# Sliding-window attention and a two-layer product on one core: the written order of steps is replaced, the steps of both products get explicit names, and chunk 1 of the first layer uses its three PSUM banks turned by one

## The chip, the cores and the metric

The kernel runs on one core of one Trainium2 chip. The metric is device time in microseconds (us) of one execution, lower is better. Three runs of the kernel before gave 321.90, 321.86 and 319.94 us; their median is 321.86 us.

## The reference

```python
# q, k, v: (8 batches, 8 heads, 576 tokens, 64)
scores = q @ k^T / 8
mask = (rel >= 0) & (rel < 64)            # rel = query position - key position
attn = softmax(where(mask, scores, -1e9))
x = (attn @ v) as (4608 tokens, 512)      # heads side by side
h = x @ w_in                              # w_in: 512 x 2048
y = (h - tanh(h)) @ w_out                 # w_out: 2048 x 512
```

All of it is float32 outside; the matrix products run in bf16 with float32 sums in PSUM.

## The kernel before

**Work.** Heads are handled in pairs: pair `g` (0 to 31) is two heads of batch `g // 4`. A window is 64 tokens; a batch has nine. The tokens of all batches stand in one row of 72 windows, cut into nine chunks of eight (512 tokens). A batch therefore ends inside a chunk: batch 4 supplies the last four windows of chunk 4 and the first five of chunk 5.

**Order.** Nothing is scheduled by the framework. A text, `PLAN`, is a list of words; `play` goes through it from left to right and issues each step on its engine. Each engine runs its own queue in that order and waits only for semaphores, so the text fixes the order on every engine, and the place of a word matters only against the other words of the same engine. The waits follow from the tiles: a step waits for what writes what it reads, and also for earlier steps that still use what it overwrites. The overlap is judged by the tile's region, and it counts by the place in the text: a fill that stands behind a load into the same tile waits for the load's landing, one that stands before the load does not.

The words that this document uses:

- `lk.g.p`, `lq.g.p`, `LQ.b`, `lr.b.i.h`, `LV.b.i`, `lv.b.pr.half`, `lt.b`, `wi.i`, `wo.i`: loads issued by GpSimd (POOL): keys and queries of a pair, queries of a batch, key rows of block `i` of a batch, rows of V, parts of V of batch 1, the two weight matrices. `lk.0.s` and `lq.0.s` go by SyncE (SP). Loads of POOL use eight semaphores in turn, so each waits until the one eight places before it has landed.
- `mv.i` fills the ones column and the empty first block of V buffer `i` (`vw`); `mk`, `mt`, `mq`, `h`, `i`, `n`, `z` fill other constants; `z` clears two large query buffers `qz` on POOL (`more_zeros`).
- `za`, `zb` and `Z.b` copy V across the partition halves (`Z` is two copies on VectorE, `cross_rows`). `cz.g` copies queries into `qz` (POOL), `bo.g` writes them to DRAM, `td.g` and `tk.b.i` are transposing DMAs of SP that give queries and keys.
- `ck`, `cq` cast keys and queries; `Fp`, `Ep` transpose them on TensorE; `Fc`, `Ea`, `Eb`, `Ec` take them out of PSUM. The last letter of such a word is the engine: `a` ScalarE, `v` VectorE, `p` GpSimd.
- `Rp.g.grp.bank` are scores, `Rx` their exponential (ScalarE), `M.g` the mask on the result (VectorE), `P`/`PP` the product with V for one or two pairs, `D` or `DR`, `DN` the division by the sum (VectorE).
- `Xp`, `Xc` transpose a batch's result into the chunk tiles by TensorE (batches 0 to 2); from batch 3 on `Y.b` does it by two transposing DMAs of SP, one for each chunk that the batch lies in.
- `H.c.m` is one of 16 blocks of the first layer for chunk `c` (four matmuls of 128x512, `hp_mm`), `A` its tanh on ScalarE (`squash`), `G` the subtraction on VectorE (`g_sub`). `W.c.s.part` is a quarter of the second layer for 128 tokens (`yp_mm`), `O.c.s` the copy out and the store (`y_out`). Before the change these five words carry no numbers: `step` counts how often each has come up and takes the next block.

**PSUM.** `ps` has eight banks. The first layer uses banks 0, 1 and 2 in chunks 0 and 1 and banks 0 and 1 from chunk 2 on, so `H` waits for the subtraction of the block two or three places earlier. The second layer uses banks 2 and 0 in chunk 0, bank 2 in chunks 1 to 7, banks 0 and 2 in the last. Scores use bank 4 (for the first four pairs 0, 1 and 4, 7), transposes banks 2 and 3, products with V banks 5 to 7.

Of the kernel before, what the change touches and what calls it, by code (L numbers as in the profile page):

```python
# [15 lines left out]
def kernel(  # L16
# [10 lines left out]
    B, H, S, D = q.shape  # L27
# [452 lines left out]
    FIRST = [(0, m, s) for s in range(2) for m in range(SPLIT)] + [(0, m, None) for m in range(SPLIT, M)]  # L480

# [3 lines left out]
    def hp_mm(c, m, s):  # L485
        n = columns(s)
        hp = ps[:, m % 2 if c > 1 or s is not None else m % 3, n]
        for ki in range(4):
            nc.tensor.matmul(hp, w_in_tile(ki, m),  # L489
                             chunk_tile(c)[:, n.start // 64:n.stop // 64, ki % 2, 64 * (ki // 2):64 * (ki // 2) + 64],  # L490
                             start=(ki == 0), stop=(ki == 3))
        return hp
# [15 lines left out]
    def yp_mm(c, st):  # L508
        s, part = divmod(st, 4)
        if c == 0:  # L510
            s, part = 2 * (st // 8) + st % 2, st % 8 // 2
        if c == NC - 1 and s == 3:
            half = part // 2
            d = slice(half * (d_model // 2), (half + 1) * (d_model // 2))
            for m in range(8 * (part % 2), 8 * (part % 2) + 8):
                nc.tensor.matmul(ps[:, 2 - half, d], gT[c][:, m, s * 128:(s + 1) * 128], w_out_sb[:, m, d],  # L516
                                 start=(m == 0), stop=(m == M - 1))
            return
        yp = ps[:, yp_bank(c, s), :]
        for i in range(4):  # L520
            m = 4 * part + i
            nc.tensor.matmul(yp, gT[c][:, m, s * 128:(s + 1) * 128], w_out_sb[:, m, :],  # L522
                             start=(m == 0), stop=(m == M - 1))
# [31 lines left out]
    def first_layer():
        k = step("H")
        hidden[k] = hp_mm(*k)

    def tanh():
        k = step("A")  # L560
        hidden[k] = squash(k[2], hidden[k])

    def subtract():
        k = step("G")
        g_sub(*k, *hidden.pop(k))
# [18 lines left out]
        H=first_layer, A=tanh, G=subtract, W=lambda: yp_mm(*step("W")), O=lambda e: y_out(*step("O"), e))  # L584

    def play(script):
# [103 lines left out]
```

## Time and profile before

| what | value |
|---|---|
| runs | 321.90, 321.86, 319.94 us, median 321.86 |
| span of the profiled execution | 317.8 us, so 4.1 us less than the median run |
| mean granted TensorE clock | 0.995 |
| TensorE matmul busy | 305.3 us (96%), 2412 matmuls |
| VectorE, ScalarE, GpSimd busy | 187.8, 173.2, 111.7 us |
| first layer (L489) | 576 matmuls, 140.2 us busy |
| second layer (L522) | 560 matmuls, 135.9 us busy |
| DMA | 39.11 MB, engines at 90% or more in nearly all of the first half |

The page shows one execution. Its span runs from the first to the last instruction; no time of its own is printed for that execution, and what a run takes beyond the span is start and end, the 4.1 us above. A busy TensorE does not mean a TensorE at its peak, since matmuls overlap: two matmuls of 128x512 that follow each other start 0.216 us apart, though each is listed with 0.379 us. How long TensorE really stood is therefore read from the starts of its instructions.

### The profile page before, as it was taken

How to read it: one execution, taken by the hardware profiler on the slowest of the kernel's cores; microseconds unless marked ns; L12 is line 12 of the kernel's file. 1: busy time of each engine (PE TensorE's matmuls, PEld its weight loads, DVE VectorE, ACT ScalarE, POOL GpSimd, SP SyncE). 2: the span in 40 equal slices, each digit the busy share in tenths (PEclk: the TensorE clock that was granted, in tenths of full speed). 3: DMA queues.
4: the chain of work that ended last, by engine and by line, in shares of the span. 5: the costliest groups of instructions: out<-in, count | busy, mean ns of one | idle time of the engine just before them, and what ended most of it. 6: DMA issues, size and time to landing. Idle time of an engine off the chain costs nothing.

```text
span 317.8 us, 6105 instructions
## 1 busy us (share of the span) xinstructions
PE 305.3 (96%) x2412; PEld 165.7 (52%) x2412; DVE 187.8 (59%) x321; ACT 173.2 (54%) x322; POOL 111.7 (35%) x164
## 2 busy tenths in 40 slices
PE   7878999999999999999799999999999999999995
PEld 2455565656655655555455555555554544445444
DVE  2355995489887896769374666566753554244400
ACT  4678885589778675555344635544524435334311
POOL 8982849985871384892021430000000000000000
PEclk9799999999999999999999999999999999999999
DMA  9999999999999699999998999262014010010021
GB/s 151 152 202 198 190 196 130 181 154 146 155 138 166 99 138 151 188 148 119 199 156 157 136 166 206 72 144 72 33 36 107 33 68 33 33 36 33 33 99 68
DMA packets 113133, 39.11 MB, mean 123 GB/s; under 512 B 96336, under 2 KB 107600, under 8 KB 113104
## 3 DMA queue, kind: packets, MB, share of 16 engines
q0 software_dynamic: 72064, 18.06, 66.4%
q1 hardware_dynamic: 41040, 20.65, 31.4%
q8 instruction: 19, 0.31, 0.4%
q14 instruction: 10, 0.08, 0.1%
HBM read 36.70 MB, written 11.80 MB: 153 GB/s over the span
## 4 chain that ended last, share of the span: by engine, by line
PE 86%; DMA 5%; DVE 4%; ACT 3%; issue 1%; SPq 0%; ACTq 0%; DVEq 0%
PE ps L489 37%; PE ps L522 36%; PE ps L300 4%; DMA xT<-xs 3%; PE ps L261 3%; PE ps L418 3%; PE ps L225 1%; DMA qf<-in_q_dram 1%; PE ps L516 1%; DVE xs L447 1%; PE ps L453 1%; ACT qt L88 1%; DVE qt L90 1%; DVE vw L167 1%; ACT pt L305 1%
## 5 line engine op out<-in xcount | busy, mean ns | idle before, releaser
L489 PE MATMUL ps<-xT,wi 128*128 128x512 bf16 x576 | 140.2, 379 | 2.4 <-DMA xT<-xs 1.7
L503 DVE TENSOR_TENSOR gT<-ps,th 128x512 bf16<-128x512 f32 x144 | 97.9, 689 | 72.5 <-ACT th L497 68.3
L522 PE MATMUL ps<-w_out_sb,gT 128*128 128x512 bf16 x560 | 135.9, 379 | 0.0
L497 ACT ACTIVATE th<-ps 128x512 f32<-128x512 f32 x144 | 85.3, 598 | 74.7 <-PE ps L489 70.9
L489 PEld LDWEIGHTS <-wi 128*128 128x128 bf16 x576 | 62.6, 113 | 53.6 <-DMA xT<-xs 1.8
L522 PEld LDWEIGHTS <-gT 128*128 128x128 bf16 x560 | 52.9, 98 | 55.3
L305 ACT ACTIVATE pt<-ps 128x384 bf16<-128x384 f32 (+1 forms) x92 | 46.0, 504 | 24.5 <-PE ps L300 23.0
L176 POOL DMA_DIRECT2D kall<-in_k_dram x50 | 37.2, 753 | 11.0 <-DMA vw<-in_v_dram 4.7
L160 POOL DMA_DIRECT2D vw<-in_v_dram x35 | 30.1, 866 | 12.3 <-PE ps L300 11.9
L88 ACT ACTIVATE ysb<-ps 128x512 f32<-128x512 f32 (+1 forms) x25 | 14.6, 582 | 29.4 <-PE ps L522 26.8
L393 DVE TENSOR_TENSOR pt<-pt,ps 128x1152 bf16<-128x1152 bf16 x28 | 20.7, 746 | 4.0 <-ACT pt L305 4.0
L128 POOL COPY qz<-qall 96x384 bf16<-96x384 bf16 x16 | 7.6, 517 | 41.4 <-DMA qd<-qz 35.7
L300 PEld LDWEIGHTS <-kw 128*128 128x128 bf16 x180 | 14.3, 98 | 10.9
L300 PE MATMUL ps<-qt,kw 128*128 128x128 bf16 x180 | 19.7, 219 | 0.0
L88 ACT ACTIVATE qt<-ps 64x576 bf16<-64x576 bf16 x25 | 16.1, 643 | 3.0 <-PE ps L300 1.5
L438 DVE TENSOR_TENSOR xs<-ps,rcp 128x384 bf16<-128x384 f32 x28 | 15.1, 552 | 0.3
L90 DVE COPY qt<-ps 64x576 bf16<-64x576 bf16 x15 | 11.3, 755 | 3.5 <-PE ps L261 2.0
L90 DVE COPY ysb<-ps 128x512 f32<-128x512 f32 x12 | 8.2, 685 | 7.9 <-PE ps L522 7.9
L418 PEld LDWEIGHTS <-pt 128*64 128x64 bf16 x504 | 9.2, 111 | 4.6 <-issue 2.4
L225 PE MATMUL ps<-warm 128*128 128x512 bf16 x25 | 10.1, 552 | 1.3 <-DVE warm L206 1.1
L418 PE MATMUL ps<-vw,pt 128*64 128x65 bf16 x504 | 10.7, 197 | 0.4 <-DVE vw L167 0.4
L261 PE MATMUL ps<-ident,qb 96*128 96x96 bf16 x132 | 9.6, 210 | 0.4 <-DVE qb L90 0.3
(68 smaller groups left out, 167.6 us busy)
## 6 DMA issues: line engine op xcount, KB each, us to landing
out_dram<-ysb SPq DMA_DIRECT2D x35, 256.0 KB, 2.3
vw<-in_v_dram POOLq DMA_DIRECT2D x28, 128.0 KB, 5.9
qall<-in_q_dram POOLq DMA_DIRECT2D x5, 576.0 KB, 8.9
kall<-in_k_dram POOLq DMA_DIRECT2D x40, 64.0 KB, 5.8
qd<-qz SPq DMA_DIRECT2D x8, 288.0 KB, 4.1
w_out_sb<-in_moe_w_out_dram POOLq DMA_DIRECT2D x4, 512.0 KB, 8.5
kall<-in_k_dram POOLq DMA_DIRECT2D x11, 144.0 KB, 5.1
qall<-in_q_dram POOLq DMA_DIRECT2D x11, 144.0 KB, 5.2
```

The costliest lines, as they stand in the source:

```text
L88: nc.scalar.activation(o, i, ACT.Copy)
L90: eng.tensor_copy(o, i)
L160: nc.gpsimd.dma_start(out=w[:, 2 * i + 1, :, 0:D] if i < NF else w[64:128, 2 * i, :, 0:D], in_=v[b, :, 128 * i:128 * i + n].rearrange("h p ...
L176: nc.gpsimd.dma_start(out=token_rows(b)[0:c, i, :, h, :], in_=k[b, NP * h:NP * h + NP, 128 * i:128 * i + c].rearrange("r p d -> p r d"))
L300: nc.tensor.matmul(sp[:, i], kt[:, 64 * j:64 * j + 128], qT[g % NR][:, :, 64 * j:64 * j + 64], start=first, stop=first or i == n - 1)
L305: nc.scalar.activation(PT[g % NPT][:, js[0]:js[0] + len(js), :].rearrange("p i (h t) -> p i h t", h=2), sp, ACT.Exp, scale=scale)
L393: nc.vector.tensor_tensor(p, p, mask.unsqueeze(1).to_broadcast([128, 2 * NJ, 64]), ALU.mult)
L418: nc.tensor.matmul(ps[r, bank, 65 * i:65 * i + 65], PT[(g + r2) % NPT][:, j, r], vw[b % 2][:, j, p0 + r2 + NP * h, :], start=True, stop=True)
L489: nc.tensor.matmul(hp, w_in_tile(ki, m), chunk_tile(c)[:, n.start // 64:n.stop // 64, ki % 2, 64 * (ki // 2):64 * (ki // 2) + 64], start=( ...
L497: nc.scalar.activation(th[:, n], hp, ACT.Tanh)
L503: nc.vector.tensor_tensor(gT[c][:, m, columns(s)], hp, th, ALU.subtract)
L522: nc.tensor.matmul(yp, gT[c][:, m, s * 128:(s + 1) * 128], w_out_sb[:, m, :], start=(m == 0), stop=(m == M - 1))
```

## The change

`FIRST`, `count` and `step` go. `H`, `A`, `G`, `W` and `O` carry their block's numbers, so blocks may come out of order (`H.2.1` before `H.2.0`). In `yp_mm`, the matmul that starts or ends a sum is found by counting the quarters that have come up, not by the number of the block. In chunk 1 the bank of block `m` is `(m + 1) % 3` instead of `m % 3`. The words of `PLAN` get a new order throughout; 56 words change between ScalarE and VectorE. The set of matmuls, loads, copies and stores is otherwise the same.

```diff
-        hp = ps[:, m % 2 if c > 1 or s is not None else m % 3, n]
+        hp = ps[:, m % 2 if c > 1 else (m + c) % 3, n]
...
-    def yp_mm(c, st):
-        s, part = divmod(st, 4)
-        if c == 0:
-            s, part = 2 * (st // 8) + st % 2, st % 8 // 2
+    def turn(*key):
+        begun[key] = begun.get(key, 0) + 1
+        return begun[key]
+
+    def yp_mm(c, s, part):
...
-                             start=(m == 0), stop=(m == M - 1))
+                             start=n == 1 and i == 0, stop=n == 4 and i == 3)
...
-        lk.0.s lq.0.s u U.11 mq.0 mt.1 mv.0 lk.3.p i lk.1.p mt.0 cq.0.a ck.0.a Fp.0.2 Fc.0.2.a ck.1.a U.3
-        Fp.1.2 lq.1.p cq.1.a mq.1 Ep.0.3 Ec.0.3.a Fc.1.2.v LV.0.3 LV.0.1 LV.0.4 LV.0.2 U.4 Ep.1.3 Ec.1.3.a h
-        U.4 Rp.1.1.4 Rx.1.1.4 LV.0.0 Rp.1.0.0 lq.3.p lk.2.p Fp.3.2 Rx.1.0.0 Rp.0.1.4 Fc.3.2.a Rx.0.1.4
-        Rp.0.0.0 mv.1 Z.0 lq.2.p U.2 Ep.3.3 Ec.3.3.a Rx.0.0.0 U.1 Fp.2.2 Rp.3.1.4 Ep.2.3 lk.4.p lk.5.p
-        lk.7.p lq.5.p wi.0 lq.4.p n lq.7.p P.0 ck.5.v Fc.2.2.a Rx.3.1.4 Ec.2.3.a D.0 Rp.3.0.0 Fp.5.3
...
-        lk.6.p wi.2 lq.6.p lv.1.0.1 lv.1.1.0 lv.1.0.0 lt.1 lv.1.1.1 P.3 Eb.5.3.v Rp.5.0.4 D.3 Fp.4.3
...
-        tk.5.1 LQ.5 LV.4.0 LV.4.3 lr.5.3.1 LV.4.2 LV.4.1 Rx.15.1.4 Eb.17.3.a A H W Ep.16.3 G Rp.17.0.4 A
...
-        Ep.19.3 Rp.18.1.4 W A G H H cq.20.a Rx.18.1.4 Ea.19.3.a A Z.4 PP.16 Eb.19.3.v G Rp.19.2.4 Y.3
-        lr.6.1.1 lr.6.0.0 LV.5.4 LV.5.2 lr.5.0.0 lr.6.1.0 lr.6.2.1 LQ.6 lr.5.4.1 z lr.6.0.1 cz.24 lr.6.4.0
+        lk.1.p u lq.1.p cq.1.v ck.1.a LV.0.1 U.1 U.4 U.2 U.11 lq.0.s lk.3.p i Ep.1.3 cq.0.a mt.1 Ec.1.3.v lq.3.p
+        lk.0.s mt.0 Fp.1.2 LV.0.2 h Fc.1.2.a ck.0.v U.3 Rp.1.0.0 Ep.0.3 LV.0.0 mq.0 Rx.1.0.0 LV.0.3 Ec.0.3.v
+        Fp.0.2 Fc.0.2.a U.4 Rp.1.1.4 LV.0.4 lq.2.p Rx.1.1.4 lk.5.p Ep.3.3 lk.2.p Ec.3.3.a Rp.0.0.0 mv.0 Fp.3.2
+        lq.5.p Fc.3.2.v Rp.0.1.4 Rx.0.0.0 Rp.3.0.0 Rx.0.1.4 Rp.3.1.4 Rx.3.0.0 lk.4.p Ep.2.3 lq.4.p Z.0 Rx.3.1.4
+        ck.5.v P.0 lk.6.p Ec.2.3.a Fp.5.3 Fp.2.2 lq.6.p D.0 cq.5.v n Fc.5.3.a P.1 Ep.5.3 D.1 lv.1.0.0 Fc.2.2.a
...
+        H.0.0 H.0.1 A.0.0 wi.2 cq.6.v A.0.1 Eb.4.3.v G.0.0 Rp.4.2.4 G.0.1 Rx.4.2.4 lq.7.p H.0.2 H.0.3 lq.8.p
+        ck.6.v A.0.2 Rp.4.0.4 G.0.2 Fp.7.3 A.0.3 Fc.7.3.v lv.1.0.1 lv.1.1.0 wo.0 H.0.4 G.0.3 mv.1 H.0.5 A.0.4
+        Rx.4.0.4 G.0.4 Fp.6.3 A.0.5 G.0.5 H.0.6 Rp.4.1.4 Fc.6.3.v lv.1.1.1 A.0.6 H.0.7 H.0.8 G.0.6 lk.8.p lt.1
+        A.0.7 A.0.8 Rx.4.1.4 H.0.9 cq.7.v zb.1.0.p G.0.7 Ep.7.3 A.0.9 G.0.8 Ea.7.3.a H.0.10 wo.1 Eb.7.3.a A.0.10
...
+        O.0.2.v Ep.10.3 H.1.0 Rx.8.1.4 Rp.9.0.4 LV.2.3 Eb.10.3.a cq.12.a A.1.0 lr.3.0.1 Rx.9.0.4 LV.2.4
...
+        tk.4.2 Rx.13.2.4 lr.6.3.1 H.2.3 lr.5.4.1 H.2.2 Ea.14.3.a z A.2.3 Rp.13.0.4 W.1.1.1 Rx.13.0.4 G.2.3
...
+        Rx.14.0.4 G.2.2 W.1.1.2 Eb.15.3.v LQ.5 H.2.4 Z.3 W.1.1.3 A.2.4 Rp.15.2.4 A.2.5 Ep.17.3 Rx.15.2.4 PP.12
...
+        W.1.3.2 Rx.16.2.4 Rp.16.1.4 W.1.3.3 G.2.13 H.2.14 Y.3 tk.5.1 Eb.18.3.a Ea.18.3.a Ep.19.3 lr.5.2.0
+        Rx.16.1.4 O.1.3.v lr.5.0.0 A.2.14 Rp.18.1.4 W.2.0.0 tk.5.4 M.17 W.2.0.1 H.2.15 Ea.19.3.v G.2.14 H.3.0
+        Eb.19.3.a M.16 A.2.15 Z.4 A.3.0 lr.7.1.1 Rx.18.1.4 G.2.15 W.2.0.2 G.3.0 H.3.1 cq.22.v Rp.19.2.4 A.3.1
+        PP.16 tk.5.3 H.3.2 G.3.1 A.3.2 H.3.3 Rx.19.2.4 W.2.0.3 DR.16 G.3.2 A.3.3 Rp.18.0.4 LV.5.1 H.3.4 LV.5.3
+        G.3.3 lr.5.0.1 lr.7.4.1 Rx.18.0.4 tk.5.2 O.2.0.v DN.16.1 LQ.6 Rp.19.1.4 DN.16.2 A.3.4 H.3.5 Rx.19.1.4
...
+        W.2.1.0 lr.6.3.0 H.3.6 G.3.5 W.2.1.1 cq.21.a lr.6.2.1 Rx.18.2.4
...
+        W.2.2.1 Z.5 Rx.20.0.4 A.3.9 G.3.9 LV.6.2 H.3.10 A.3.10 Rp.21.1.4 H.3.11 Rx.21.1.4 A.3.11 W.2.2.2
...
+        Rx.23.0.4 DR.20 tk.6.4 W.2.3.3 Rp.23.2.4 O.2.3.v DN.20.0 H.4.0 LV.6.0 td.25 Rx.23.2.4 A.3.15 DN.20.2
```

## The prediction

> **What bounds the kernel now.** First the page and its chain that ended last.
>
> ```profile
> span 317.8 us, 6105 instructions
> ...
> PE 86%; DMA 5%; DVE 4%; ACT 3%; issue 1%; SPq 0%; ACTq 0%; DVEq 0%
> ```
>
> TensorE (PE) carries 86% of the chain, so the question is where it stands. The chain in order of time shows the two places that matter:
>
> ```profile
> 28.53 2.59 PE ps L489 x12
> ...
> 142.30 10.54 DMA xT<-xs
> 152.89 1.05 PE ps L489 x4
> ...
> 310.78 3.51 PE ps L516 x32
> ```
>
> The first layer begins only at 28.4 us; and at 152.89 `H.4.0` has waited for a transposing DMA of `Y.4` issued at 142.30.
>
> To see the rest I give each step a place: the TensorE work that the text puts ahead of it, by starts of one matmul to the next (0.216 us at 512 columns, so 0.86 for an `H` or `W`; about 0.17 for scores, 0.25 for a transpose group, 0.76 for `PP`). All work is 297.7 us. A step's start less its place is the lag, and it grows only where TensorE stands: `H.0.0` 28.4 - 16.5 = 11.9; `H.1.0` 64.05 - 51.4 = 12.65; `H.3.0` 119.24 - 104.9 = 14.3; `H.4.0` 152.89 - 136.6 = 16.3; last matmul 314.3 - 297.7 = 16.6. After 160 us the kernel is TensorE without gaps. The change keeps the work and nearly every place (`H.1.0` 51.3, `H.3.0` 105.7, `H.4.0` 137.4), so it can act only on the lag: 11.9 at the start, 4.7 behind it. About 1.5 to 2 of these 4.7 are 0.1 us steps around `PP`, which stay.
>
> **The change part by part.**
>
> *The start.* `lk.1` and `lq.1` go first, and casts are split over two engines. In order through the new text with the durations of the timeline (cast 0.84 on ScalarE, 0.35 on VectorE; copy out of PSUM 0.65 and 0.76; exponential 0.6 to 0.7): `cq.1` at 6.45, `Ep.1` 7.25, scores of pair 1 done at 9.15, against 12.6 to 14 now. `ck.0.v` from float32 has no row on VectorE; it lies between 0.35 (bf16) and 0.84 (ScalarE), and it moves nothing by more than 0.2. But `mv.0` now stands behind `LV.0.0` to `LV.0.4`, writes into their tile, and so waits on VectorE for the landing of all. Nine POOL loads land by then, and the ninth does so at 13.94 in the trace (issued 9.10, 4.8 to landing). Behind it on VectorE stand `Fc.3.2`, `Z.0` and `ck.5`:
>
> ```profile
> 13.57 0.70 DVE L166 COPY vw<-vw 64x2080 bf16<-64x2080 bf16 x1 [2.66 <-DMA vw<-in_v_dram]
> 14.28 0.79 DVE L167 COPY vw<-vw 64x2080 bf16<-64x2080 bf16 x1
> ```
>
> These two are `Z.0` now, done at 15.07. After: `mv.0` 14.05 to 14.85 (0.8, as at 1.88 now), `Fc.3.2` to 15.6, `Z.0` to 17.1, two us later than now. From there the chain `P.0`, `D.0`, `P.1`, `D.1`, `ck.4` (0.85 on ScalarE), `Rx.2`, `P.2`, `D.2`, `Xc` runs with fewer gaps than now and gives `H.0.0` at 27.0 (now 28.4).
>
> Then the second fill. `mv.1` stands behind `lv.1.1.0` and waits for its landing; `G.0.4` stands behind `mv.1`, and `H.0.7` needs the bank that `G.0.4` frees.
>
> ```profile
> L189 POOL DMA_DIRECT2D wi<-in_moe_w_in_dram x1: 767/767/767, 18.1 to 18.1; - x1
> DMA to landing us min/median/max: 12.7/12.7/12.7
> ```
>
> ```profile
> L147 POOL DMA_DIRECT2D vw<-in_v_dram x1: 750/750/750, 22.4 to 22.4; - x1
> DMA to landing us min/median/max: 11.7/11.7/11.7
> ```
>
> `wi.2` lands at 30.8 and the fourth load behind it at 34.1, 3.3 later. In the new order the same bytes and 0.4 us more lie ahead of `wi.2`, and `lv.1.1.0` is the fourth behind it: 31.3 + 3.3 = 34.6. `mv.1` to 35.4, `G.0.4` to 36.1, `H.0.7` at 36.15; TensorE could have begun it at 34.1. Now it begins at 35.43, so the lead is gone and 0.7 lost. Next ScalarE is the narrow one: from `A.0.7` to `A.0.15` it has nine tanh (5.4), four exponentials (2.0), `Ea.7`, `Eb.7`, `Ea.6` (1.95) and `ck.8` (0.84), 10.2 us over 8.3 us of TensorE. `W.0.0.0` needs bank 2, freed by `G.0.14`: 47.2 against 45.54 now. I take +1.7; between -1.0 (`lv.1.1.0` at 33 and nothing crowded) and +2.5.
>
> *The gate of TensorE's clock* also speaks in the start:
>
> ```profile
> 5.60:9.10 3.50, 1.82 (x21) 0.95 (x21) 0.00 (x0) 2.98 (x5) 3.35 (x8) 0.99 1.93 146
> 9.10:12.50 3.40, 3.40 (x18) 1.62 (x16) 1.37 (x3) 1.51 (x3) 3.40 (x7) 0.50 3.06 124
> 12.50:15.90 3.40, 3.13 (x59) 1.73 (x58) 1.49 (x2) 2.33 (x4) 3.02 (x7) 1.00 1.29 181
> ```
>
> (stretch, TensorE busy, ..., granted clock, DMA share, GB/s.) After a stretch with 1.82 of 3.5 us busy the clock is half for one stretch. After the change TensorE waits for `Fc.3.2` from 13.55 to 15.65, so I expect half clock from 15.9 to 19.3, which costs 0.6 on `P.0` and the transposes; it is in the 27.0. The Trainium skill (TensorE: Matmul & The Clock Gate, What's actually happening) has the clock fall after an idle window of about 3.4 us; by that rule a window that is half busy would keep it, and the start would be 0.6 better. The row shows the fall at half busy, so I go by the row.
>
> *The bank of chunk 1.* `H.1.0` waits 0.47 (start to start) for the copy of bank 0 by `O.0.3`. With bank 1 first, last read by `G.0.13`, that wait goes: -0.5, at worst 0.
>
> *`z` and `Z.4`.* Here is what stops TensorE around 118:
>
> ```profile
> 115.19 1.93 POOL L235 MEMSET qz<- 96x1536 bf16 x1
> 115.81 1.86 DVE L167 COPY vw<-vw 64x2080 bf16<-64x2080 bf16 x1
> 117.72 0.76 PE L418 MATMUL ps<-vw,pt 128*64 128x65 bf16 x36 [0.37 <-DVE vw L167]
> 119.24 0.59 PE L489 MATMUL ps<-xT,wi 128*128 128x512 bf16 x2 [0.40 <-DVE gT L503]
> ```
>
> `Z.4` takes 0.93 + 1.86 under POOL's fill, 1.5 at `Z.0`. `PP.16` waits 0.53 and `H.3.0` 0.56. After the change `z` runs near 87, beside copies out of PSUM, and `PP.16` stands 1.9 of place behind `Z.4` (now 0). `G.2.15` behind `Z.4` may cost 0.25. So -0.85, between -1.1 and 0. The Trainium skill (GPSIMD Engine Reference, Specifications) says that POOL shares its SBUF interface with VectorE's two-port copies; if that holds for any such pair, `z` must miss `Z.3` as well, or 1.3 comes back there; `Z.3` runs near 97, so I count nothing.
>
> *`H.2.4`.* It needs `G.2.2`, whose tanh stands behind `Rx.14` and ends near the place 82.1; +0.6, between 0 and +1.0.
>
> *`lr.7.1.1` on POOL.* It overwrites the rows that `tk.5.1` reads, and stands ahead of `LV.5.1`. `tk.5.1` stands on SP behind `Y.3`, which waits for `DN.14.1` (place 99.4, about 114 us), so POOL stands until about 119.5: two transposes of 1.2 and 1.7, one of 1.2, 1.3 to landing. Now it stands at the same point for `PP.14`, to 108.6:
>
> ```profile
> POOL vw L160 <- PE ps L300: 11.9, 1, 11.9
> ```
>
> So the rest of the loads starts 11 us later. Behind it: `LV.5.1`, `LV.5.3`, two key rows, `LQ.6` (landed 10 later, by the bytes), `cz.24` (0.95, waits for `LQ.6`), `LV.5.0`, `LV.5.2` (landed near 136). `Z.5` needs them at place 124.7, about 139. Three us of cover: 0, and up to +5 without it.
>
> *`Y.4`.* `DN.18.1` ends near 145.5, SP does `bo.25` and `tk.6.3` (1.25) first, `Y.4` is issued at 146.3. Now 10.5 us to landing, with `LQ.7` in flight; later rows take 3.6 and 2.3. In the new order POOL then waits in `cz.27` for `bo.25` and `LQ.7` is far behind, so I take 4, landed at 150.3, and `H.4.0` needs it at 152. The 1.8 of now would go; half trusted, -1.2; between -1.8 and +2.5.
>
> *Late.* `PP.24` comes 2.9 of TensorE behind `H.4.15`, and tanh, `G` and `Z.6` in between take 2.7: +0.3, up to +0.8. The other chains of chunks 4 to 8 have 0.14 us or more to spare, as now.
>
> Sum: +1.7 - 0.5 - 0.85 + 0.6 + 0 - 1.2 + 0.3 = +0.05. Span 317.85; with the 4.1 that the median run has over the span, 322.0.
>
> **The rivals.**
>
> *POOL's stand decides (slower).* For it: 11 us less for the loads, and in the stretch after 108.6 `LQ.6` took until 123.6, 15 us, beside `Y.3` and `tk.5`. At 15 us `LV.5.2` lands near 141.4, `Z.5` is 2.4 late, and `G.3.9` behind it holds `H.3.11` without cover; `LV.5.4`, which the new text puts behind `LV.6.2`, is late for `PP.20` in turn, another 1 to 3. Against it: `Y.3` is through by then. It decides from 3 us of lateness on; price +4, 326.
>
> *The start costs more (slower).* If `wi.2` slips by 1.5 us, `mv.1`, `lv.1.1.1` (which waits for `mv.1` on POOL), `wo.1` and `wo.3` slip with it; together with `Y.4` still late, +3.5, 325.5.
>
> *The start holds (faster).* `H.0.0` at 26, `lv.1.1.0` at 33, tanh keeps up: -1.0, with -0.5, -1.1 and -1.8, 317.5. Against it: nothing lets four loads behind `wi.2` land in 2 us.
>
> *The order does nothing*, since TensorE is full anyway: 321.9 - 0.5 = 321.4. It is the same outcome as mine.
>
> **How the numbers follow.** A measurement of this kernel tells about 1% (3.2 us) from no change. My forecast with the last rival 0.44 (within 1%; its own range is 319 to 325), POOL's stand 0.19, the start 0.14, the start that holds 0.23. Faster 0.23, same 0.44, slower 0.33. Low end: the low bounds together, -4.4, and 1.5 of the spread of the runs: 316. High end: +2.5 of the start, +2.5 of `Y.4` and +3 of POOL: 330.
>
> **What would show it.** In the timeline after: `mv.0` (L209) ending a wait for `vw` loads near 14; `H.0.0` near 27; `mv.1` near 34.6 and `H.0.7` standing about 2 us; no wait at `H.1.0`; `Z.4` in 1.5 us; POOL's longest wait ended by `kw` (`tk.5.1`) near 119; no wait for `xT` at `H.4.0`. Wrong would be: `H.0.7` without a wait, `Z.5` waiting for `vw`, or a lag at `W.0.0.0` off by over 1 us from 13.7.

## The result, and the profile after

The changed kernel takes 332.36 us (median of 333.17, 333.69, 330.0 and 331.55) against 320.9 us for the kernel before (the median of three executions on record and a fourth of 318.86), a ratio of 1.0353 with a 95% interval of 1.0287 to 1.0419. It is slower by 3.5%; the prediction was 322.0, with 330 as the upper end of its range. The profiled execution is the one of 333.17 us, with a span of 331.4 us, 13.6 more than before; the medians differ by 11.5. From here on a median is over all executions of a kernel, while a ratio with its interval leaves out executions that are over 1.5% above the fastest of the same kernel.

From the page of the kernel after, the span and the chain that ended last, by engine:

```profile
span 331.4 us, 6084 instructions
...
PEclk9959799999999999989999699999999999999999
...
PE 66%; DMA 16%; POOL 8%; DVE 4%; issue 2%; ACT 1%; POOLq 0%; DVEq 0%; ACTq 0%
```

TensorE (PE) carried 86% of the chain before and carries 66% now; transfers went from 5% to 16%, POOL came in with 8%. The clock row, 8.3 us to a digit, has four dips that were not there: a 5 from 17 us on, a 7 from 33, an 8 from 141 and a 6 from 182. The chain in order of time names the transfers:

```profile
22.33 13.22 DMA vw<-in_v_dram
...
126.13 9.09 DMA qall<-in_q_dram
137.24 6.04 DMA vw<-in_v_dram
...
171.69 11.06 DMA qt<-qd
```

They are the load `lv.1.1.0`, the loads `LQ.6` and `LV.5.2`, and the transpose `td.24`. Where each of them holds TensorE is read with the prediction's measure, the lag: the start of a step less its place (the TensorE work that the text puts ahead of it). The last column is the lag before plus the terms of the prediction's sum that act up to that step.

| step | lag before | lag after | forecast |
|---|---|---|---|
| `H.0.0` | 11.9 | 10.5 | 10.5 |
| `H.0.15` | 12.0 | 15.8 | 13.7 (at `W.0.0.0`) |
| `H.1.0` | 12.6 | 15.8 | 13.8 |
| `H.3.0` | 14.4 | 16.7 | 15.3 |
| `H.3.15` | 14.5 | 21.6 | 15.4 |
| `H.4.0` | 16.3 | 21.7 | 16.0 |
| `H.4.15` | 16.4 | 30.0 | 16.1 |
| `H.8.0` | 16.5 | 30.1 | 16.6 |

30.1 - 16.5 is the whole 13.6. There are three jumps: 5.3 between `H.0.0` and `H.0.15`, 5.0 within chunk 3, 8.3 within chunk 4. Everywhere else the new order keeps its lag as well as the old one, within 0.2, or better.

Each jump is a wait and then a stretch at half clock. In the table by stretch, laid on the boundaries at which the granted clock changes (us; TensorE busy; weight loads; VectorE; ScalarE; POOL; granted clock; DMA share; GB/s):

```profile
34.21:37.62 3.41, 0.38 (x2) 0.23 (x2) 1.58 (x4) 0.43 (x1) 1.34 (x2) 1.00 0.35 66
37.62:41.04 3.42, 3.42 (x9) 1.18 (x8) 2.39 (x5) 1.12 (x3) 3.33 (x7) 0.50 1.24 102
143.44:146.85 3.41, 1.20 (x6) 0.63 (x6) 3.17 (x5) 0.34 (x2) 3.41 (x6) 1.00 1.73 110
146.85:150.26 3.41, 3.41 (x15) 1.58 (x13) 1.46 (x3) 0.95 (x2) 2.43 (x4) 0.50 1.11 71
177.57:180.98 3.41, 0.00 (x0) 0.00 (x0) 0.21 (x1) 0.00 (x0) 0.00 (x0) 1.00 1.60 121
180.98:184.39 3.41, 1.59 (x7) 0.75 (x7) 0.00 (x0) 0.49 (x1) 1.03 (x3) 0.50 2.42 189
184.39:187.81 3.42, 3.42 (x10) 1.18 (x9) 1.16 (x2) 0.60 (x1) 0.82 (x2) 0.50 1.73 66
```

At 34.21, 143.44 and 177.57 TensorE is busy for 0.38, 1.20 and 0.00 of 3.41 us. The stretch behind each runs at half clock. In such a stretch (37.62 to 41.04) matmuls of 128x512 start 0.427 us apart, against 0.216 at full clock, so half of the busy time there is lost: 1.7 us where the stretch is full. At 180.98 TensorE waits on for 1.8 us with the clock already half, so the 1.59 us of work there cost 0.8, and a second, full stretch at half clock follows: 2.5 together.

**The first jump** is the start's second fill. In the timeline of VectorE (start, us, engine, line; the idle time and what ended it in brackets):

```profile
31.87 0.68 DVE L501 TENSOR_TENSOR gT<-ps,th 128x512 bf16<-128x512 f32 x1
35.87 0.12 DVE L209 MEMSET vw<- 128x72 bf16 x1 [3.32 <-DMA vw<-in_v_dram]
36.15 0.49 DVE L210 MEMSET vw<- 64x520 bf16 x1 [0.17 <-DVE vw L209]
36.57 1.22 DVE L501 TENSOR_TENSOR gT<-ps,th 128x512 bf16<-128x512 f32 x2
```

`mv.1` (L209, L210) waits for a value load and `G.0.4` stands behind it; `H.0.7` begins at 37.24 and has waited 3.23 us (start to start).

**The second** is POOL's stand. In the table of waits (engine, line, waited for; us in total, times, longest), and then in POOL's timeline:

```profile
POOL kall L176 <- DMA kw<-kall: 13.2, 1, 13.2
...
PE ps L487 <- DVE gT L501: 5.9, 2, 3.1
...
PE ps L300 <- DMA qt<-qd: 5.7, 1, 5.7
```

```profile
122.02 0.92 POOL L176 DMA_DIRECT2D kall<-in_k_dram  x1 [13.19 <-DMA kw<-kall]
122.93 1.86 POOL L160 DMA_DIRECT2D vw<-in_v_dram  x2
124.78 1.39 POOL L176 DMA_DIRECT2D kall<-in_k_dram  x2
126.13 0.82 POOL L114 DMA_DIRECT2D qall<-in_q_dram  x1
...
135.34 0.94 POOL L128 COPY qz<-qall 96x384 bf16<-96x384 bf16 x2 [6.27 <-DMA qall<-in_q_dram]
136.36 1.76 POOL L160 DMA_DIRECT2D vw<-in_v_dram  x2
```

`lr.7.1.1` waits 13.19 us for `tk.5.1`. `LQ.6` is issued at 126.13 and lands at 135.2; `cz.24` stands behind its landing on POOL, and `LV.5.0` and `LV.5.2` behind `cz.24`. `LV.5.2` lands at 143.28, `Z.5` runs then, and the bank that `G.3.9` frees behind `Z.5` comes 3.02 us late.

**The third** is a collision. `LV.7.4` holds POOL 11.08 us, until `PP.22` is through; then everything queued behind it leaves at once, `LQ.7` (L114, 576 KB) half a microsecond after SP has issued `td.24` at 171.69:

```profile
171.07 0.72 POOL L160 DMA_DIRECT2D vw<-in_v_dram  x1 [11.08 <-DVE rcp L426]
172.17 0.78 POOL L114 DMA_DIRECT2D qall<-in_q_dram  x1 [0.39 <-issue]
172.95 3.33 POOL L160 DMA_DIRECT2D vw<-in_v_dram  x4
```

The line of `td` (L138), with the time from issue to landing:

```profile
L138 SPq DMA_TRANSPOSE qt<-qd x8: 1227/1513/2230, 160.3 to 231.6; - x8
...
  PE ps L300: 5.7, 1
...
DMA to landing us min/median/max: 3.1/3.9/11.1
```

The median is 3.9 us; `td.24` takes 11.1 and `Rp.24.1` waits 5.87.

What became better is there too. `H.4.0` has no wait for `Y.4`, and `z` is out of `Z.4`'s way (timeline of the kernel after; before, the fills took 1.38 and 1.93 and the copies 0.93 and 1.86):

```profile
93.50 2.69 POOL L235 MEMSET qz<- 96x1536 bf16 x2
...
121.94 0.70 DVE L166 COPY vw<-vw 64x2080 bf16<-64x2080 bf16 x1
122.65 0.79 DVE L167 COPY vw<-vw 64x2080 bf16<-64x2080 bf16 x1
```

### The profile page after: what moved, and what is told of

Same layout as the page of the kernel before. It is cut to its first block, busy times and chain, and to the rows that moved or that the text cites. A ratio compares the mean times of both kernels' runs of the same rounds, so it can differ in the third digit from the quotient of the medians.

```text
span 331.4 us, 6084 instructions
## 1 busy us (share of the span) xinstructions
PE 310.6 (94%) x2383; PEld 169.0 (51%) x2412; DVE 190.6 (58%) x330; ACT 169.2 (51%) x313; POOL 111.4 (34%) x164
## 4 chain that ended last, share of the span: by engine, by line
PE 66%; DMA 16%; POOL 8%; DVE 4%; issue 2%; ACT 1%; POOLq 0%; DVEq 0%; ACTq 0%
PE ps L526 30%; PE ps L487 29%; DMA qall<-in_q_dram 6%; DMA vw<-in_v_dram 6%; DMA qt<-qd 3%; PE ps L300 3%; PE ps L418 2%; DVE gT L501 2%; POOL qall L108 2%; POOL vw L160 2%; POOL kall L108 2%; POOL kall L176 1%; PE ps L519 1%; DMA kall<-in_k_dram 1%; DVE vw L167 1%
## 5 line engine op out<-in xcount | busy, mean ns | idle before, releaser
L487 PE MATMUL ps<-xT,wi 128*128 128x512 bf16 x576 | 144.3, 384 | 6.1 <-DVE gT L501 5.9
L495 ACT ACTIVATE th<-ps 128x512 f32<-128x512 f32 x144 | 84.4, 597 | 90.4 <-PE ps L487 86.5
L526 PEld LDWEIGHTS <-gT 128*128 128x128 bf16 x560 | 53.7, 99 | 58.4 <-issue 3.0
L305 ACT ACTIVATE pt<-ps 128x384 bf16<-128x384 f32 (+2 forms) x92 | 45.8, 503 | 36.0 <-PE ps L300 32.4
L160 POOL DMA_DIRECT2D vw<-in_v_dram x35 | 30.1, 866 | 15.9 <-DVE rcp L426 11.1
L88 ACT ACTIVATE ysb<-ps 128x512 f32<-128x512 f32 (+1 forms) x22 | 12.7, 577 | 19.9 <-PE ps L526 14.3
L88 ACT ACTIVATE qt<-ps 64x576 bf16<-64x576 bf16 x27 | 17.3, 641 | 5.7 <-DVE qt L90 2.2
L90 DVE COPY qt<-ps 64x576 bf16<-64x576 bf16 x13 | 9.8, 755 | 5.3 <-PE ps L300 2.7
L90 DVE COPY ysb<-ps 128x512 f32<-128x512 f32 x15 | 10.3, 686 | 3.9 <-PE ps L526 3.8
L147 POOL DMA_DIRECT2D vw<-in_v_dram x8 | 6.2, 785 | 13.7 <-DVE vw L209 10.7
L261 PEld LDWEIGHTS <-qb 96*128 96x128 bf16 x132 | 7.9, 99 | 3.8 <-issue 0.4
## 6 DMA issues: line engine op xcount, KB each, us to landing
qall<-in_q_dram POOLq DMA_DIRECT2D x5, 576.0 KB, 10.3
```

What stands on the lines that cost most here:

```text
L88: nc.scalar.activation(o, i, ACT.Copy)
L90: eng.tensor_copy(o, i)
L160: nc.gpsimd.dma_start(out=w[:, 2 * i + 1, :, 0:D] if i < NF else w[64:128, 2 * i, :, 0:D], in_=v[b, :, 128 * i:128 * i + n].rearrange("h p ...
L305: nc.scalar.activation(PT[g % NPT][:, js[0]:js[0] + len(js), :].rearrange("p i (h t) -> p i h t", h=2), sp, ACT.Exp, scale=scale)
L487: nc.tensor.matmul(hp, w_in_tile(ki, m), chunk_tile(c)[:, n.start // 64:n.stop // 64, ki % 2, 64 * (ki // 2):64 * (ki // 2) + 64], start=( ...
L495: nc.scalar.activation(th[:, n], hp, ACT.Tanh)
```

## The experiments

### Each of the three steps moved alone, and all together

`r1_mv1_head`, `r2_lr711_behind_lq6` and `r3_lq7_early` move one step each in the changed kernel; `r4_all_three` has all three moves.

```diff
 # r1
-... lv.1.1.0 wo.0 H.0.4 G.0.3 mv.1 H.0.5 A.0.4 ...
+lk.1.p u mv.1 lq.1.p ...
 # r2
-... Z.4 A.3.0 lr.7.1.1 Rx.18.1.4 ...
+... DN.16.1 LQ.6 lr.7.1.1 Rp.19.1.4 ...
 # r3
-... G.4.6 A.4.7 G.4.7 LQ.7 H.4.8 LV.6.4 ...
+... DN.20.1 cz.27 LQ.7 tk.6.1 lr.7.4.0 ...
```

> The changed kernel with one step moved: mv.1 (VectorE's two fills of the second value tile) goes back to the head, where VectorE is idle, instead of behind the load lv.1.1.0. Theory (a stall costs itself and, behind it, TensorE at half clock): H.0.7 loses its wait of 3.23 us and the 3.41 us at half clock behind it (1.7), so TensorE is 4.9 us ahead from 41 us on, and the median is about 332.4 - 4.9 = 327.5 (ratio to the kernel before 1.020). The waits for Z.5 (3.0) and td.24 (5.9) stay as they are. Rival (the loads set the pace): POOL's lv.1.1.1 is now early too, but what TensorE wins in front it gives back at Z.5 and at td.24, whose data come when the DMA engines have them: the two waits grow by up to 4.9 together and the median stays at 331 to 332.5 (ratio 1.032 to 1.036).

Measured: 325.5 us, ratio 1.010 (1.0009 to 1.0192), 6.9 below the changed kernel where 4.9 were expected. The 325.5 is the median of 321.14, 324.93, 326.07 and 326.71, and the ratio rests on the first two, so the size is known to some 2 us only; all four lie below the rival's time. `H.0.7` has no wait and the clock is full there. `Z.5` is still late, but by 2.12 instead of 3.02, and no half clock follows; `Rp.24.1` waits 5.76. The theory holds in its direction, the rival does not.

> The changed kernel with one load moved: lr.7.1.1, which on POOL waits 13.2 us for the transfer tk.5.1, goes behind LQ.6 instead of ahead of LV.5.1. Theory: LV.5.1 is issued near 109 to 113 instead of 123, LQ.6 lands near 126 instead of 135, LV.5.0 and LV.5.2 land by 136, and Z.5's wait of 3.02 us and the 3.41 us at half clock behind it (1.7) go: 332.4 - 4.7 = 327.7 (ratio 1.021). Rival (the bytes collide anyway): LQ.6 now flies beside the transposes of Y.3, makes them late as it made them in the kernel before, H.3.0 or a score of pair 19 waits 2 to 5 us, and the median is 330 to 334 (ratio 1.03 to 1.04).

Measured: 327.4 us, ratio 1.0234 (1.0185 to 1.0283): the time as expected, but not by the path that I gave. POOL's timeline:

```profile
112.91 1.76 POOL L160 DMA_DIRECT2D vw<-in_v_dram  x2 [2.71 <-PE ps L418]
114.66 0.77 POOL L176 DMA_DIRECT2D kall<-in_k_dram  x1
125.70 0.62 POOL L176 DMA_DIRECT2D kall<-in_k_dram  x1 [10.27 <-DVE qb L90]
126.31 0.79 POOL L114 DMA_DIRECT2D qall<-in_q_dram  x1
```

POOL stands again, one load further on: `lr.7.4.1` overwrites rows that `tk.5.4` has to read (the line's releaser names another engine, whose work is not what this load needs; `tk.5.4` lands at 125.2). `LQ.6` is issued at 126.31, no sooner than before. But `LV.5.1`, `LV.5.3` and one row load have gone ahead of the stand, which fits fewer bytes in flight beside `LQ.6` (not shown apart from the rest): it lands at 132.8 instead of 135.2, `LV.5.2` at 140.0 instead of 143.3, and `Z.5` is in time. It was the 3 us of landing that mattered, not the place of the stand.

> The changed kernel with one load moved: LQ.7 (576 KB) goes on POOL from behind LV.7.4, which waits for PP.22, to right behind cz.27, so it is issued near 157 instead of 172. Theory (td.24 is late because the 576 KB of LQ.7 went ahead of it through the same DMA engines): td.24 takes 2 to 4 us to landing instead of 9.2, the wait of 5.87 us at Rp.24.1 goes, and so do the 6.83 us at half clock (3.4): 332.4 - 9.3 = 323.1 (ratio 1.007). Rival 1 (td.24 is slow by itself or by the four LV loads that stay beside it): its landing still takes 8 us or more, and the median stays at 331 to 333. Rival 2 (the collision only moves): LQ.7 lands near 168 and makes td.25 or a tk.6 late by as much; a score of pair 25 waits 3 to 6 us, and the median is 327 to 333 (ratio 1.02 to 1.04).

Measured: 326.6 us, ratio 1.0154 (1.0096 to 1.0213): by the medians 5.8 of the 9.3 won. `td.24` now takes 6.3 us and nobody waits for it; but `LQ.7`, issued at 154.87 and landed at 163.3, has the four row loads behind it in flight until 168, and `tk.6.0`, issued at 164.37, lands at 170.2. The table of waits of this kernel has

```profile
PE ps L300 <- DMA kw<-kall: 4.0, 2, 2.8
```

(the longer one 2.8, 3.01 start to start, with 3.41 us at half clock behind it). Both the theory and rival 2 are half right: the 576 KB were the larger part of the cause, and part of the price moved to the next transpose. They were not all of it: with `LQ.7` and five value loads beside it `td.24` took 11.1 us (the changed kernel), 10.3 (`r1`), 10.9 (`r2`) and 10.3 (`r5`); with the value loads alone 6.3 (`r3`), 7.6 (`r4`) and 7.3 (`r8`); the median of its line is 3.9. So `LQ.7` stands for 3 to 5 us of it, and the value loads for the rest.

> The changed kernel with the three moves together: mv.1 at the head, lr.7.1.1 behind LQ.6, LQ.7 right behind cz.27. Theory (three late data and the half clock behind each are all that the new order lost): 332.4 - 4.9 - 4.7 - 9.3 = 313.5, below the kernel before (ratio 0.977). Rival (what the order wins in front the loads take back behind): 319 to 325 (ratio 0.995 to 1.013), with new waits of 2 us and more in the trace.

Measured: 320.32 us, ratio 0.9996 (0.9964 to 1.0027). So these three steps, of a plan of 1,269, hold the whole loss of 3.5%. The clock is full from 23 us on. The expected 313.5 does not come: waits of 2.21 (`Rp.25.0`, for `tk.6.0`) and 2.05 (`Rp.24.1`, for `td.24` beside five `LV` loads) are there, 4.3 of the 6.8 us that are missing; the other 2.5 stay open. The start has 6.83 us at half clock, but so has the start of the changed kernel, so that is no reason for the difference.

### The half clock by itself

`r5_fill_stall` leaves the order as it is and keeps TensorE at work in the third wait.

```diff
-... Rx.25.1.4 LV.7.1 Rp.24.1.3 ...
+... Rx.25.1.4 LV.7.1 U.27.3 Rp.24.1.3 ...
```

> The changed kernel with 27 idle matmuls of 512 columns (27 x 0.216 = 5.8 us, on the zero tile that the start uses) put ahead of Rp.24.1, in the place where TensorE waits 5.87 us for td.24. Theory (the half clock behind a wait is caused by the wait itself, TensorE being idle): the clock stays at 1.00 from 150 us to the end, the 6.83 us at half clock do not come, and the median falls by 3.4 to 329.0 (ratio 1.025), although the kernel does more work. Rival (the clock falls for another reason, or the fill delays TensorE beyond td.24): no gain, median 332 to 334 (ratio 1.035 to 1.04).

Measured: 327.63 us, ratio 1.0242 (1.0154 to 1.033). The stretches of this kernel around the wait (columns as above):

```profile
170.30:173.70 3.40, 3.40 (x18) 1.68 (x16) 2.03 (x5) 2.52 (x5) 2.45 (x3) 1.00 1.17 105
173.70:177.10 3.40, 3.40 (x18) 1.51 (x17) 0.56 (x1) 0.00 (x0) 0.00 (x0) 1.00 1.23 154
177.10:180.50 3.40, 3.35 (x19) 1.68 (x19) 0.00 (x0) 0.52 (x2) 1.85 (x4) 1.00 1.86 197
```

`td.24` lands at 179.14, and `Rp.24.1` starts behind the 27 matmuls at 179.24: the same wait, filled with work that nobody needs, and the clock stays. From `H.4.9` to `H.4.11` the lag grows by 5.8 us here and by 8.3 in the changed kernel, so the filling saved 2.5, the size of the half clock in the table above. The rest of the 4.7 us is not the filling's: in this execution `H.0.7` waited only 0.47 (3.23 in the changed kernel, 2.36 in `r2` and 3.00 in `r3`, whose starts are in the same order), behind a start that was itself later (`H.0.0` at 28.21), and `Z.5` was 1.88 late, with full clock behind it. The 3.4 expected was too much, since the first of the two stretches at half clock holds only 1.59 us of work.

The runs also say how much idle time it takes. In the steady part of the kernels a stretch of 3.41 us with TensorE busy for 1.23 us or less was followed by half clock each time, and one at full clock with 1.38 or more never. The nearest two, of `r13_tk62_ahead` and of `r11_z_early_in_before` below:

```profile
148.51:151.92 3.41, 1.38 (x32) 0.85 (x27) 2.87 (x6) 1.54 (x4) 0.33 (x1) 1.00 1.05 84
151.92:155.34 3.42, 0.00 (x0) 0.00 (x0) 0.68 (x2) 0.00 (x0) 3.42 (x6) 1.00 2.46 141
```

```profile
150.25:153.67 3.42, 1.23 (x16) 0.55 (x16) 0.69 (x1) 0.60 (x2) 0.00 (x0) 1.00 1.39 145
153.67:157.08 3.41, 3.19 (x41) 1.68 (x37) 0.69 (x1) 1.51 (x3) 0.00 (x0) 0.50 1.09 271
```

(In the first pair the stretch with 1.38 us keeps the clock, although nothing is done in the one behind it; half clock comes only after that one, from 155.34.) So idle time of 2.2 us that lies within one stretch costs up to 1.7 more, and a wait of 2.97 that is split over two (in `r10_y4_cq12` below, with TensorE busy for 1.70 in the one and 2.16 in the other) costs nothing more. The Trainium skill (TensorE: Matmul & The Clock Gate, What's actually happening) has free-running windows of 3,413 ns, which these stretches agree with; its fall after an idle window does not need a wholly idle one here.

### What else can be had from the new order

```diff
 # r8 = r4 and mv.0 at the head behind mv.1
 # r6 = r8, but LQ.7 behind LV.7.3, and td.24 ahead of tk.7.3
 # r7 = r8, but LQ.7 behind LV.6.2, and td.24 ahead of tk.7.3
+lk.1.p u mv.1 mv.0 lq.1.p ...
+... W.2.2.1 Z.5 Rx.20.0.4 A.3.9 G.3.9 LV.6.2 LQ.7 H.3.10 ...      # r7
+... Rp.22.0.4 lr.7.0.1 td.24 tk.7.3 ...                          # r6, r7
+... td.27 LV.7.3 LQ.7 cz.28 ...                                  # r6
```

> r4_all_three with one more step moved: mv.0 to the head of VectorE, so that Fc.3.2 no longer stands behind its wait for the value loads. Theory: the wait of 1.7 us near 14 goes and with it the 6.83 us at half clock behind it (up to 3.4): H.0.0 at 22 to 24 instead of 26.8, median 320.3 - 1.7 to 4 = 316 to 318.6 (ratio 0.988 to 0.995). Rival 1 (the clock falls anyway, since TensorE is less than half busy before 17 us): only 1 to 1.7 is won, 318.6 to 319.3. Rival 2 (the loads set the pace behind): TensorE comes earlier to the waits at Rp.25.0 and Rp.24.1 and the median stays at 320.

Measured: 321.58 us in four runs from 316.6 to 322.89, too wide for an interval. The trace tells more: `H.0.0` at 25.15 (27.08 in `r4_all_three`) and no half clock in the start; but the waits behind are `H.4.0` 1.03, `Rp.25.0` 2.10, `Rp.25.1` 0.81 and `Rp.24.1` 2.50, where `r4_all_three` had 2.21 and 2.05. In the execution of the trace (321.71 us) that is rival 2: what the start wins, late transfers take back. Another execution took 316.6, so it need not be so each time. Nor does the start always keep the clock with `mv.0` and `mv.1` at the head: of the seven kernels that have them there, the profiled executions of `r6_lq7_last` (3.41 us from 17.22) and `r13_tk62_ahead` (6.83 us from 18.80) show half clock in the start.

> r4_all_three with mv.0 at the head too, LQ.7 behind LV.7.3 (the last of the five LV loads) instead of behind cz.27, and td.24 ahead of tk.7.3 on SP. Theory (what is left in r4_all_three is 2.2 us at Rp.25.0 behind LQ.7, 2.05 us at Rp.24.1 beside the LV loads, and 1.7 us plus half clock at Fc.3.2): all go, 320.3 - 4.3 - 1.7 to 4 = 310.5 to 314.5 (ratio 0.97 to 0.98). Rival (LQ.7 hits whatever follows it on SP): it is issued near 167 and lands near 177; td.27 or Y.5 is late, and a score of pair 27 or H.5.0 waits 2 to 6 us: 315 to 321 (ratio 0.985 to 1.00).

Measured: 319.24 us, ratio 0.9932 (0.9876 to 0.9988). `td.27` and `Y.5` are in time, against the rival; but `Rp.25.1` waits 3.02 us for `tk.6.2`, which SP now issues behind `td.24` and `tk.7.3`, and 3.41 us at half clock follow.

> As r6_lq7_last, but LQ.7 goes forward to right behind LV.6.2 (near 135 us, ahead of the ten loads of batches 6 and 7 that follow). Theory (a free stretch for LQ.7 is where no transpose of SP follows within 10 us): it lands near 145, before Y.4 is issued, and the time is as good as r6_lq7_last or better: 310.5 to 314.5 (ratio 0.97 to 0.98). Rival: the loads behind it come 7 to 10 us later, LV.5.4 is late for PP.20 or tk.6.3 and Y.4 are late as in the kernel before: 314 to 322 (ratio 0.98 to 1.005).

Measured: 317.42 us, ratio 0.9904 (0.9855 to 0.9954), faster than both kernels. `LQ.7` is issued at 134.2 and lands at 141.5, before `Y.4` is issued at 144.65; no half clock anywhere. It is 1.0% and not the 2 to 3% of the theory: `H.1.3` waits 1.49, `H.4.0` 1.32 (for `Y.4`, beside the eight loads behind `LQ.7`), and TensorE is idle for 2.4 us in small pieces ahead of `H.0.0` (at 24.44).

### Parts of the change alone

The bank of chunk 1, in `r7_lq7_first`:

```diff
-        hp = ps[:, m % 2 if c > 1 else (m + c) % 3, n]
+        hp = ps[:, m % 2 if c > 1 else m % 3, n]
-... PP.10 G.1.13 tk.3.0 ...
+... PP.10 G.1.13 G.1.14 tk.3.0 ...
```

> r7_lq7_first with the PSUM banks of chunk 1 as in the kernel before (m % 3), and G.1.14 moved up to right behind G.1.13, since W.1.0.0 then writes the bank that G.1.14 reads. Theory (the turned bank takes away the wait of H.1.0 for bank 0): H.1.0 waits 0.3 to 0.5 us (start to start) for the copy of O.0.3, as in the kernel before, and the rest is as in r7_lq7_first. Rival (in the new order O.0.3 stands two steps ahead of H.1.0, and the turn is there for W.1.0.0): H.1.0 has no wait over 0.1 us in either numbering, and a wait, if any, appears at W.1.0.0.

Measured, in one execution of 317.29 us (TensorE's timeline; `H.1.0` is the line at 61.17, `W.1.0` the one at 82.55):

```profile
60.92 0.41 PE L261 MATMUL ps<-ident,qb 96*128 96x96 bf16 x6
61.17 1.03 PE L487 MATMUL ps<-xT,wi 128*128 128x512 bf16 x4
...
81.82 0.34 PE L300 MATMUL ps<-qt,kw 128*128 128x128 bf16 x3
82.55 1.02 PE L526 MATMUL ps<-w_out_sb,gT 128*128 128x512 bf16 x3 [0.39 <-DVE gT L501]
```

`H.1.0` begins without a wait in the old numbering as well, and the wait is at `W.1.0` (0.55 start to start). The rival holds: the order took away the wait of `H.1.0`, by putting `O.0.3` further ahead, and the turn of the bank is what lets `W.1.0.0` begin ahead of `G.1.14`.

`z` in the kernel before:

```diff
-... LQ.6 lr.5.4.1 z lr.6.0.1 cz.24 ...
+... LV.3.2 lr.5.2.0 lr.5.3.0 z Ep.14.3 ...
```

> The kernel before with one part of the change alone: z (POOL's two fills of qz) goes forward from beside Z.4 to behind lr.5.3.0, near 94 us. Theory: Z.4's two copies on VectorE take 0.70 and 0.70 to 0.79 instead of 0.93 and 1.86, the fills 1.38 each instead of 1.38 and 1.93, and the waits at PP.16 (0.53) and H.3.0 (0.56) go or shrink below 0.2. Rival (the waits are the data's, not the copies'): the copies are short, and PP.16 waits as before.

Measured, in one execution of 320.65 us (VectorE's timeline):

```profile
115.04 0.70 DVE L166 COPY vw<-vw 64x2080 bf16<-64x2080 bf16 x1
115.75 0.69 DVE L167 COPY vw<-vw 64x2080 bf16<-64x2080 bf16 x1
```

The copies are short and neither `PP.16` nor `H.3.0` waits over 0.25 us, as the theory says. The time does not show it: TensorE comes to `H.4.0` that much sooner, and waits 2.36 there for `Y.4` instead of 1.82, with 3.41 us at half clock behind.

`LQ.7` in the kernel before:

```diff
-... td.24 lr.7.0.1 LQ.7 LV.6.4 ...
+... bo.25 O.a A H LQ.7 LV.5.1 lr.7.1.1 ...
```

> The kernel before with one load moved: LQ.7 from behind lr.7.0.1 (issued 0.1 us ahead of Y.4, at 142.2) forward to ahead of LV.5.1 (near 136). Theory (Y.4's 10.5 us to landing are LQ.7's bytes): Y.4 lands within 5 us of its issue, the wait of 1.82 us at H.4.0 goes, and the median falls by 1.8: 318.4 (ratio 0.994). Rival 1 (the bytes are only shifted: the nine loads behind LQ.7 now fly when Y.4 does): Y.4 takes 8 us or more, H.4.0 waits 1 to 2.5 as before, ratio 0.998 to 1.004. Rival 2 (LV.5.1 and LV.5.4 come 7 us later and Z.5 is late for PP.20): a wait of 2 to 4 us near 150 to 156, ratio 1.005 to 1.015.

Measured: 317.88 us, ratio 0.9935 (0.9903 to 0.9968), 1.95 below the kernel before in the same runs. `Y.4` is issued at 142.84, its first part lands at 148.3 (10.5 us before, 5.5 now), and `H.4.0` (at 151.60) follows without a wait:

```profile
151.44 0.33 PE L300 MATMUL ps<-qt,kw 128*128 128x128 bf16 x3
151.60 1.03 PE L489 MATMUL ps<-xT,wi 128*128 128x512 bf16 x4
```

So `LQ.7` alone made `Y.4` late, and this one word of the plan is worth 0.65% without any new order.

### Three more moves that gave nothing clear

```diff
 # r12 = r7 and cq.12 behind A.1.0
-... Eb.10.3.a cq.12.a A.1.0 ...
+... Eb.10.3.a A.1.0 cq.12.a ...
 # r10 = r12 and tk.6.3 behind Y.4
-... Eb.23.3.v tk.6.3 lr.7.2.0 ... G.3.14 Y.4 PP.20 ...
+... Eb.23.3.v lr.7.2.0 ... G.3.14 Y.4 tk.6.3 PP.20 ...
 # r13 = r12 and tk.6.2 ahead of td.24
+... lr.7.0.1 tk.6.2 td.24 tk.7.3 ...
```

> r7_lq7_first with two steps moved for the two waits that are left in its trace behind the start: cq.12 behind A.1.0 on ScalarE (it stood 1.42 us there for LQ.3's landing, and H.1.3 stood 1.49 for the bank), and tk.6.3 behind Y.4 on SP (it took 2.24 us there, and H.4.0 stood 1.32 for Y.4). Theory: both waits go, span 314.5 - 2.8 = 311.7, median 317.4 - 2.8 = 314.6 (ratio 0.982). Rival (both hang on the landing of loads that come no sooner): cq.12's wait then holds A.1.2 or Ea.11, Y.4 waits for DN.18.1 instead, and the median stays at 316.5 to 317.5 (ratio 0.988 to 0.992).

Measured: 318.88 us, ratio 0.992 (0.9877 to 0.9963). The wait at `H.1.3` goes. `Y.4` is issued at 141.79 instead of 144.65 and lands at 151.45, later than the 150.27 of `r7_lq7_first`; `H.4.0` waits 2.97. `Y.4` took 9.7 us here. In `r7`, `r12` and `r14` `LQ.7` had landed 2.2 to 3.2 us before `Y.4` was issued, and `Y.4` took 5.1 to 5.6; here `LQ.7` landed (at 143.4) 1.6 us after the issue. So what was won by the sooner issue fits being lost to `LQ.7`, still in flight; five executions with `r13` below agree, which is not a proof.

> r7_lq7_first with cq.12 behind A.1.0 alone; tk.6.3 stays ahead of Y.4. Theory (a transpose is quick when the loads ahead of it are through, not when it is issued soon): H.1.3's wait of 1.49 goes as in r10_y4_cq12, H.4.0's wait for Y.4 is 1.3 to 1.9 as in r7_lq7_first and not 3.0, and the median is 1 to 1.5 below r7_lq7_first: 316 (ratio 0.986). Rival (what is won ahead of Y.4 is given back there, since Y.4 lands when the loads let it): H.4.0 waits 2.5 to 3 us, and the median is 317.4 again (ratio 0.990 to 0.993).

Measured: 318.51 us, ratio 0.9941 (0.99 to 0.9981). `H.4.0` waits 1.02, as the theory says, and `H.1.3` not at all; but `Rp.25.1` waits 2.62 for `tk.6.2`, a place that neither side had named.

> r12_cq12 with tk.6.2 ahead of td.24 on SP (it stood behind td.24, tk.7.3 and a store). Theory (each transpose costs SP 1.2 us and lands 1.2 to 3 us later, so the order on SP decides who is late): the wait of 2.62 us at Rp.25.1 goes, td.24 is issued 1.2 later and still lands before Rp.24.1, span 315.8 - 2.6 = 313.2, median 318.5 - 2.6 = 315.9 (ratio 0.986). Rival (the transposes stand in the DMA engines): td.24 or tk.7.3 is late in its place, a wait of 2 us or more stays near 162 to 172, median 318 to 319 (ratio 0.992 to 0.996).

Measured: 317.15 us, ratio 0.9897 (0.9858 to 0.9936). The profiled execution took 322.73, far above the median; in it `Rp.25.1` has no wait, and `H.4.0` waits 5.49 for `Y.4`, with `LQ.7` landing at 145.3, 0.3 behind the issue of `Y.4`. There are also 6.83 us at half clock in the start and 3.41 from 155.34 on. `r7`, `r10`, `r12` and `r13` have intervals that overlap, so which of them is best is not settled. From its issue to its landing `Y.4` takes 5.6 us in `r7`, 5.1 in `r12` and 10.4 in `r13`, though the plan ahead of it is the same in `r12` and `r13`; why `LQ.7` lands so much later in this execution stays open.

## Why the prediction was wrong

Right, or off by less than a microsecond:

- *`H.0.0` at 27.0*: 26.95. `mv.0` waited until 13.8 (14.05 forecast), TensorE stood from 13.6 to 15.2 (13.55 to 15.65), and the clock was half from 17.1 (15.9). That the sum comes out to 0.05 is partly luck: `Z.0` was done at 16.6 and not at 17.1, and TensorE went on 0.45 sooner, while half clock lasted 6.83 us and not one stretch of 3.4.
- *`z` and `Z.4`, -0.85*: the copies take 0.70 and 0.79, and from `H.2.0` to `H.3.0` the lag grows by 0.2 where it grew by 1.2. `r11_z_early_in_before` shows that `z` is the cause. *`H.2.4`, +0.6*, lies in the same stretch and cost nothing to be seen: a term that was wrong, and small.
- *`Y.4`, -1.2*: no wait at `H.4.0`, so the full 1.8 was won. `r14_lq7_in_before` shows that `LQ.7` beside `Y.4` was what had made it late, the reason that the prediction gave and trusted by half.
- *The bank, -0.5*: the wait is gone, but by the order and not by the bank (`r9_bank_back`): the right number with the wrong reason.
- *Late, +0.3*: nothing; from `H.5.0` on the lag grows by 0.1. This small term was wrong too.

Wrong, and these three make the result:

- *The start, +1.7*: it was +3.8 at `H.0.15`. The mechanism was as described (`mv.1` behind `lv.1.1.0`, `G.0.4` behind `mv.1`, `H.0.7` behind the bank). Its size was off twice. `lv.1.1.0` was in at 35.6, not 34.6: `wi.2` landed at 33.0, not 31.3, and the distance behind it was 2.5, not 3.3. And the wait of 3.23 brought half clock, 1.6 of lag from `H.0.8` to `H.0.15`, which the sum did not have.
- *`lr.7.1.1` on POOL, 0*: it was 5.0. This is the first rival, whose price of 4 lacked the half clock. The step that failed is the landing of `LV.5.2` near 136. The prediction ends the stand at 119.5 and lets `LQ.6` land 10 us later than before, which is some 133.6; it names `cz.24`, which waits for that landing, but behind it the copy (0.95) and the issue of two loads (0.9 each) use up the time to 136 and leave the loads none to land in. Measured: the stand ended at 122.02, `LQ.6` landed at 135.2, and `LV.5.2` was issued at 137.24 and took 6.04 us, to 143.28. The three us of cover were less than that; the wait was 3.0, and 1.9 of half clock came behind it.
- *`td.24`*: 8.3 us, and not in the sum at all. The prediction says of `LQ.7` that it is far behind `Y.4` in the new order, counts the gain of that, and stops. It did not ask which transpose stands next to `LQ.7` now. `r3_lq7_early`, `r4_all_three` and `r14_lq7_in_before` show the same 576 KB with three other victims: `tk.6.0`, `td.24` beside the loads that followed, and none.

Under all three lies one omission. The prediction read the gate of the clock in the start of the kernel before and charged it there only. Each of the three waits was over 3 us, and each brought at least one stretch at half clock: 1.6, 1.9 and 2.5 us (the jumps less their waits; the first from `H.0.8` to `H.0.15`), 6.0 of the 13.6.

One smaller thing was misread ahead of the prediction. The 4.1 us between the span of before and its median are not start and end: in every execution on record the time is 1.65 to 1.86 us above the span of the same execution (333.17 against 331.4 after). The rest is that the profiled execution of before was faster than the median one.

The last rival, that the order does nothing, was put into the same outcome as the forecast with 0.44 between them. `r4_all_three` shows what is true in it: without the three late steps the new order is worth 0.9996 of the old.

## What to carry to other kernels

When a step is moved away from a big load, the gain is half of the account: look up which transfer stands beside that load in the new order, and when its consumer needs it; and when an engine waits at the head of its queue, follow every item behind it to its consumer, not only the first. A wait of TensorE of over about 2 us can bring half clock behind it and should be priced with that; matmuls that nobody needs, put in its place, kept the clock here and saved 2.5 us. Fills of a tile (`mv`) belong where their engine is idle and ahead of the loads into that tile: behind them a fill of 0.6 us waits for a DMA.

## What the runs showed of the hardware

- A transposing DMA took nearly three times as long beside other loads: `td.24` landed 11.1 us after its issue beside `LQ.7` and five value loads, against a median of 3.9, although it was issued ahead of `LQ.7`. The Trainium skill (DMA: Bandwidth & Descriptors, Queues, rings and completion order) has each DMA engine serve its queues in turn, packet by packet. Equal shares of two queues would, as an estimate from the median, make 3.9 us into some 8; the trace has 11.1. In the packets of the trace the first row of `td.24` starts 2.3 us after the issue, its 1,152 packets of 256 B take 6.0 us, and the landing follows 2.7 us after the last; `td.30`, alone at 231.60, has 2.3, 1.4 and 0.4. So turns can account for the longer row of packets, but not for the 2.7 us behind the last; what holds the landing back there is not shown.
- In the steady part the clock falls after a stretch that is 36% busy and stays after one of 40% (1.23 and 1.38 of 3.41 us). In the start, where TensorE does small transposes and scores, it fell after stretches with 1.24 (`r2`) to 2.19 us (`r6`) busy and stayed after one of 2.08 (`r11`), so busy time alone does not tell there.
- What is won ahead of a late transfer is taken back at it, with half clock on top where the wait grows past the limit (`r11_z_early_in_before`, `r8_mv0_head`).
